# Query projection in two groups of row pairs a step, with two banks begun by their 128-row parts and the two sets of transposes in one pair of banks

## The chip, the cores and the metric

The kernel runs on one core of a Trainium2 chip. The metric is device time in microseconds (us) of one execution, as the median of several runs. The matrix engine is TensorE (PE in the profile, with PEld for its weight loads). VectorE (DVE) and ScalarE (ACT) do the elementwise work and empty the matrix engine's result banks (PSUM, eight banks). GpSimd (POOL) does a few small operations, and SyncE (SP) issues the DMAs. Each engine works through its own list of instructions in order, and semaphores tie the lists together.

## The reference

The input x has 2048 tokens of 448 numbers. A layer A (attention over segments, with a memory) and a layer B (a gated feed-forward) are applied twice in turn, each behind a layer norm and with a residual:

```python
for s in range(n_seg):                       # 64 segments of 32 tokens, one after the other
    h = concat([mem, xs])                    # 8 memory rows + 32 tokens = 40 rows
    q, k, v = h @ Wq, h @ Wk, h @ Wv         # 16 heads of 256
    p = softmax(where(mask, q @ k.T * scale, -1e9))
    o = (p @ v) @ Wo
    mem = o[:M]                              # the next segment's memory
    outs.append(o[M:])
...
x = x + A(layernorm(x)); x = x + B(layernorm(x))     # and both once more
B(x) = (max(x @ W_gate, 0) * (x @ W_up)) @ W_down
```

The memory makes each layer A a chain of 64 segments that can't run side by side. All four parts use the same weights A and B.

## The kernel before

At the start the kernel fuses Wq with Wk (tiles A_sb, A3, A3z) and Wv with Wo (B_sb) for every head. Attention then needs one "query" projection of a segment's rows, scores against the rows themselves, weighted sums of the rows (y, kept in tiles Y and Z), and one output projection (ox and o3).

**Steps.** The first A layer and the second one are two chains, the second four segments behind. `step(g, ff)` does segment g of chain 0 and segment g−4 of chain 1 together. There are 68 steps with work and a last short one. Steps 4 to 63 serve both chains (their rows stand side by side, 80 columns of a matmul); four steps at either end serve one chain (40 columns). Every second step also carries the feed-forward of a finished block (class `Feed`). In the middle of the run a step without the feed-forward takes 17.95 us and one with it 26.51 us.

**The query projection.** The 448 dims are cut into three chunks of 128 and a last one of 64. The result stands in PSUM banks named prj, class `Bank`: for each half hf of the heads (0 or 1) four banks i = 0 to 3 of six tiles each and a bank i = 4 of four tiles. I call half 0's banks b0 to b3 and z0, and half 1's c0 to c3 and z1, as the code does. Each tile takes three matmuls with all 128 rows (weights A_sb, "wide" from here on) and one with 64 rows for the last chunk (A3 or A3z). Two of the latter, on rows 0 to 63 and rows 64 to 127, run side by side on TensorE if they are issued one after the other: these are the row pairs. `open_banks` (L508) starts banks with their row pairs, and `close_bank` (L521) adds the wide matmuls and empties the bank: banks 0 to 3 go to the query tile TQ by one copy of VectorE or ScalarE, bank 4 goes to TZ in two, VectorE with partitions 0 to 63 first and ScalarE with 64 to 127.

**Other users of row pairs.** `flipped_dims` (L156) transposes with 64 rows each. It serves `hk_make` (L612), which turns the segment's rows hT into hk (eight transposes, banks kps, then copies by VectorE and ScalarE), and `Feed.residual` (L419), which turns the layer's outputs OT (eight transposes, banks otp). Of the two banks of a set, one comes from the pool tag "ox", which has one bank, and one from the pool tag "ps", which has seven and is used in turn. The output projection's bank ox has the tag "ox" as well, so a transposing set can begin only when ox has been emptied. The weighted sums y (`weigh_x`, the last thing that a step issues, 40 rows of each chain) are row pairs too.

**The end of a step.** `finish` (L736) empties ox: VectorE copies the memory columns to the next step's hT (L205), ScalarE copies the outputs of each chain to OT (L741, one copy for each chain, both on ScalarE). After it come the y matmuls of `weigh_x`, and their copies to Y or Z by both engines (L89 and L91, the lines of the helper `evac`).

**What sets the order.** On TensorE every matmul is chained to the one before (`in_order`), so that engine follows the program. On the other engines the tile framework's scheduler places the instructions, and the order in its list can differ from the program's.

The order of TensorE at the start of a step with both chains, with "|" where the form changes between row pairs and wide:

```
y, pairs of b0 b2 | wide b0, b2 | [transposes of OT, in a step with feed-forward] pairs of b1 b3 z0 z1
  | wide z0, b1, b3, z1 | transposes of hT (kps), pairs of c0 c2 c1 c3 | scores Sm of half 0, wide c0, c2, c1, c3
  transpose of the weights PM of half 0 (pps), scores Sx of half 0, weighted sum ya, ...
```

The scores Sm of half 0 need TQ and TZ of half 0. Behind them VectorE and ScalarE work out the softmax weights PM (maximum mx, difference and exponential se, sum, reciprocal, product), which TensorE transposes (pps), VectorE copies (PT), and ya reads.

Of the kernel before, what the change touches and what calls it, by code (L numbers as in the profile page):

```python
# [8 lines left out]
BF = mybir.dt.bfloat16  # L9
F32 = mybir.dt.float32  # L10
# [10 lines left out]
SEG = 32  # L21
L = MEM + SEG
# [9 lines left out]
HI = 128  # L32
HW = 5 * HI
W = 2 * L
XO = (0, 2 * L - SEG)
# [5 lines left out]
ROWS = (slice(0, 64), slice(64, 128))  # L41
# [7 lines left out]
def tidx(kd, eo, p4):  # L49

    return kd * 8 + eo * 4 + p4 if kd < 3 else 24 + p4


def build_kernel(ctx, tc, A_x, A_mem0, A_Wq, A_Wk, A_Wv, A_Wo, B_W_gate, B_W_up, B_W_down, out,
                 ntiles=16, nseg=64):
    nc = tc.nc
    P = nc.NUM_PARTITIONS
# [10 lines left out]
    psum = ctx.enter_context(tc.tile_pool(name="psum", bufs=7, space=bass.MemoryType.PSUM))  # L68
# [4 lines left out]
    def in_order(r):  # L73
        if last_pe[0] is not None:
            tc.add_manual_dep(r.ins, last_pe[0],
                              mybir.DependencyInfo(mybir.DependencyClass.NoSync,
                                                   mybir.DependencyReason.DATA),
                              reason="order of issue")
        last_pe[0] = r.ins.name

    def mm(*a, **k):
        in_order(nc.tensor.matmul(*a, **k))  # L82

    def tr(*a):
        in_order(nc.tensor.transpose(*a))  # L85

    def evac(eng, dst, src):
        if eng is nc.scalar:
            nc.scalar.copy(dst, src)  # L89
        else:  # L90
            eng.tensor_copy(dst, src)  # L91
# [8 lines left out]
    ident = glob.tile([P, P], BF, name="ident")  # L100
# [32 lines left out]
    A_sb = glob.tile([P, 3, 2, NT, 128], BF, name="A_sb")  # L133
# [5 lines left out]
    for i in range(2):  # L139
        t = glob.tile([P, BLK, HW], BF, name=f"hT{i}")  # L140
# [10 lines left out]
    for hf in range(2):  # L151
        t = glob.tile([P, 5, 6, 64], BF, name=f"TQ{hf}")
        tc.keep_in_program_order(nc.gpsimd.memset(t[:], 0.0))
        TQ.append(t)

    def flipped_dims(name, src):  # L156

        two = [psum.tile([P, 4, 64], BF, name=name, **where) for where in (dict(tag="ox", bufs=1), dict(tag="ps"))]
        for kd in range(4):
            for r in range(2):  # L160
                tr(two[r][:, kd, :], src(r, kd), ident[ROWS[r], ROWS[r]])
        return two

    def row_stats(t, pin=False):

# [220 lines left out]
    for hf in range(2):  # L386
        for name, shape, where in (("Y", [P, NT, W], YY[hf]), ("Z", [P, NT, W], YY[hf]), ("TZ", [P, 5, 128], TZ),
                                   ("PX", [P, 4, 64], PX), ("PM", [P, 2, 64], PM)):
            t = main.tile(shape, BF, name=f"{name}{hf}")
# [6 lines left out]
    OT = main.tile([P, 4, 128], BF, name="OT")  # L396
# [5 lines left out]
    for i in range(2):  # L402
        t = main.tile([P, 6, 128], BF, name=f"hk{i}")
# [4 lines left out]
    class Feed:  # L408


        def __init__(self, i):
            self.i = i
            self.first = i < nblk
            self.second = 0 <= i - LAG // BLK < nblk
            self.n = slice(0 if self.second else TB, P if self.first else TB)
            self.x = xa[i % 3]
            self.nx = xp[i % 2]

        def residual(self):  # L419
            tp = flipped_dims("otp", lambda r, kd: OT[ROWS[r], kd, :])  # L420
            xd = self.x[:].rearrange("p (c d) -> p c d", d=64)
            for r in range(2):
                nc.vector.tensor_tensor(xd[:, r::2, :], tp[r][:, 0:4 - r, :], xd[:, r::2, :], op=ALU.add)
            self.st = row_stats(self.x)
# [56 lines left out]
    def moving(hb, j, idx, chains, rows=slice(0, P)):  # L481

        if len(chains) == 2:
            return hb[rows, j, idx * HI:(idx + 1) * HI].rearrange("p (c k) -> p c k", k=64)[:, :, 0:L]
        c = chains[0]
        return hb[rows, j, idx * HI + 64 * c:idx * HI + 64 * c + L]

    class Bank:


        def __init__(self, hf, i):
            self.hf = hf
            self.i = i
            self.tiles = [tidx(kd, i // 2, 2 * (i % 2) + k) for kd in range(3) for k in range(2)] if i < 4 else                 list(range(24, NT))
            self.ps = psum.tile([P, 512], F32, tag="ps", name="prj")

        def out(self, t, n):
            k = self.tiles.index(t)
# [6 lines left out]
        kd, eo, p4 = t // 8, t // 4 % 2, t % 4  # L505
        return eo, A3[ROWS[eo], hf, 4 * kd + p4, :]

    def open_banks(chains, hb, j, *which):  # L508

        n = L * len(chains)  # L510
        banks = [Bank(hf, i) for hf, i in which]
        for a, b in zip(banks[::2], banks[1::2]):
            for k in range(len(a.tiles)):
                for bk in (a, b):
                    t = bk.tiles[k]
                    r, w = last_rows(bk.hf, t)
                    mm(bk.out(t, n), w, moving(hb, j, 3, chains, ROWS[r]), start=(k == 0), stop=False,
                       skip_group_check=True)
        return banks

    def close_bank(bk, chains, hb, j, eng):  # L521

        n = L * len(chains)
        hf, N = bk.hf, len(bk.tiles)
        for t in bk.tiles:
            for kd in range(3):
                mm(bk.out(t, n), A_sb[:, kd, hf, t, :], moving(hb, j, kd, chains), start=False, stop=(kd == 2),
                   skip_group_check=True)
        ps = bk.ps
        if bk.i < 4:  # L530
            at = 2 * (bk.i // 2) + bk.i % 2
            parts = [(eng, slice(0, P), TQ[hf][:].rearrange("p g (k b) w -> p g k (b w)", b=2)[:, :, :, 32 * at:32 * at + 32], 3)]
        else:
            parts = [(nc.vector, slice(0, 64), TZ[hf][0:64, :, 0:64].unsqueeze(2), 1),
                     (nc.scalar, slice(64, 128), TZ[hf][0:64, :, 64:128].unsqueeze(2), 1)]
        for eng, rows, T, K in parts:
            T = T.rearrange("p g k (t q) -> p k t g q", q=16)
            if len(chains) == 2:
                evac(eng, T, ps[rows, 0:N * n].rearrange("p (k t g q) -> p k t g q", k=K, t=N // K, q=16))
                continue  # L540
            c = chains[0]
            src = ps[rows, 0:N * n].rearrange("p (k t w) -> p k t w", k=K, t=N // K)
            x, m = (0, SEG) if c == 0 else (MEM, 0)
            evac(eng, T[:, :, :, 2, MEM * c:MEM * c + MEM], src[:, :, :, m:m + MEM])
            evac(eng, T[:, :, :, 3 * c:3 * c + 2, :],
                 src[:, :, :, x:x + SEG].rearrange("p k t (g q) -> p k t g q", q=16))

    def queries(hf, g, kd):
        return TQ[hf][:, g, 2 * kd:2 * kd + 2, :] if kd < 3 else TZ[hf][:, g, :]
# [47 lines left out]
    at = [0]  # L597

    def step(g, ff):
        chains = active(g)  # L600
        xs = active(g - 1)
        ms = [c for c in chains if g - c * LAG + 1 < nseg]
        gb, j = divmod(g, BLK)
        hb = hTb[gb % 2]
        cols = [(0, 32) if c == 0 else (48, 80) for c in xs] + [(32, 40) if c == 0 else (40, 48) for c in ms]
        lo, hi = min(a for a, _ in cols), max(b for _, b in cols)
        ox = None
# [1 line left out]
        def ys(hf, later=0):  # L609
            return YY[hf][(g + later) % 2]  # L610

        def hk_make():  # L612
            kps = flipped_dims("kps", lambda r, kd: hb[ROWS[r], j, kd * HI:kd * HI + HI])
            hk = HK[g % 2]
            for r, eng in enumerate((nc.vector, nc.scalar)):
                evac(eng, hk[:, 0:4, 64 * r:64 * r + 64], kps[r][:])
            nc.scalar.copy(hk[:].rearrange("p k n -> p (k n)")[:, 512:768].rearrange("p (a b) -> p a b", b=64)[:, 0::3, :],
                           kps[1][:, 3, :].unsqueeze(1).to_broadcast([P, 2, 64]))
            return hk
# [112 lines left out]
        def ot_cols(c):  # L732
            o = (g - 1) % BLK * SEG + (TB if c == 0 else 0)
            return OT[:, :, o:o + SEG]

        def finish():  # L736
            if ms:
                src = ox[:, :, M0:M0 + 16].rearrange("p k (c m) -> p k c m", m=MEM)
                set_mem(g + 1, src[:, :, ms[0]:ms[-1] + 1, :], ms, 3)
            for c in xs:  # L740
                nc.scalar.copy(ot_cols(c)[:, 0:3], ox[:, :, XO[c]:XO[c] + SEG])  # L741

        def feed(*us):
            if ff is not None:
# [3 lines left out]
        def load_some():  # L748
            if g < 3:
                for part in (2 * at[0], 2 * at[0] + 1):  # L750
                    if part < NPASS + FT // 2:
                        load_ff(part)
                at[0] += 1
# [7 lines left out]

        load_some()
        nc.gpsimd.tensor_copy(hb[ROWS[0], j, 4 * HI:4 * HI + 104], hb[ROWS[0], j, 3 * HI:3 * HI + 104])
        b0, b2 = open_banks(chains, hb, j, (0, 0), (0, 2))
        close_bank(b0, chains, hb, j, nc.vector)
        close_bank(b2, chains, hb, j, nc.scalar)
        if ff is not None:
            ff.residual()
            ff.norm(nc.gpsimd)
        b1, b3, z0, z1 = open_banks(chains, hb, j, (0, 1), (0, 3), (0, 4), (1, 4))  # L770
        close_bank(z0, chains, hb, j, None)
        load_some()
        close_bank(b1, chains, hb, j, nc.vector)
        close_bank(b3, chains, hb, j, nc.scalar)
        close_bank(z1, chains, hb, j, None)
        hk = hk_make()
        c0, c2, c1, c3 = open_banks(chains, hb, j, (1, 0), (1, 2), (1, 1), (1, 3))
        scores_m(0)
        close_bank(c0, chains, hb, j, nc.scalar)
        close_bank(c2, chains, hb, j, nc.scalar)  # L780
        close_bank(c1, chains, hb, j, nc.vector)
        close_bank(c3, chains, hb, j, nc.scalar)
# [63 lines left out]
    for g in range(nsteps + 1):  # L846
        if g == LAG - 1:
            set_mem(LAG, mem0T[:].unsqueeze(2), (1,))
        i = (g - 3) // 2
        step(g, Feed(i) if g % 2 and 0 <= i < nblk + LAG // BLK - 1 else None)  # L850

    ff = Feed(nblk + LAG // BLK - 1)
    ff.residual()
    ff.norm()
    ff.xposed()
# [62 lines left out]
```

## Time and profile before

| | us |
|---|---|
| runs shown: lowest, median, highest | 1580.89, 1584.73, 1585.72 |
| the profiled execution | 1579.01 |
| its span, from the first to the last instruction | 1576.9 |
| TensorE busy | 1547.3 |
| VectorE busy | 1112.7 |
| ScalarE busy | 783.3 |
| GpSimd busy | 174.9 |

The profiled execution took 2.1 us more than its span, and 5.7 us less than the median of the runs. The mean granted TensorE clock was 0.993 of full speed. In a list of instructions in order of time the columns are: start, time, engine, line, operation, tile written <- tiles read, shapes, and how many were merged into the row. Matmuls overlap, so the time of a group reads longer than the distance to the next group's start; the distances between starts are what counts. In the table of stages each engine has its busy time, then come the granted clock (PEclk), the DMA share and GB/s.

### The profile page before, as it was taken

Reading aid. Unit: us, or ns where it says so; the run is one execution under the profiler, and the core shown is the slowest. Engines: PE = TensorE matmul, PEld = TensorE weight load, DVE = VectorE, ACT = ScalarE, POOL = GpSimd, SP = SyncE. Lnnn points to the kernel's source line nnn. Section 1 sums busy time; section 2 is a strip of 40 time slices with the busy share of each in tenths; the row PEclk is TensorE's granted clock in tenths of the full one; section 3 lists DMA queues with packets and bytes.
Section 4 is the critical chain, followed back from the end, with each engine's and each line's share of the span. In section 5 each row is a group of like instructions: output and inputs, shape, how many; then the busy total and the mean of one; then the engine's idle time right before and its main releaser. Section 6 shows DMA issues by size and latency. Waiting matters only on the chain.

```text
span 1576.9 us, 98176 instructions
## 1 busy us (share of the span) xinstructions
PE 1547.3 (98%) x45116; PEld 1422.8 (90%) x45116; DVE 1112.7 (71%) x3825; ACT 783.3 (50%) x2307; POOL 174.9 (11%) x308
## 2 busy tenths in 40 slices
PE   8999999999999999999999999999999999999997
PEld 6588899999999999999999999999999999999886
DVE  6756777777777777777767677776777777776673
ACT  6634544554445544544445545554455545544442
POOL 3201111011001111011001111011011110111010
PEclk9989999999999999999999999999999999999999
DMA  9530000000000000000000000000000000000000
GB/s 285 149 80 9 9 10 8 6 10 10 10 10 10 10 10 8 6 9 10 10 10 10 10 10 5 8 10 10 10 10 10 10 10 5 9 8 7 7 7 6
DMA packets 29468, 33.12 MB, mean 21 GB/s; under 512 B 3320, under 2 KB 28160, under 8 KB 29056
## 3 DMA queue, kind: packets, MB, share of 16 engines
q1 hardware_dynamic: 28992, 26.85, 6.3%
q8 instruction: 352, 5.77, 1.5%
q14 instruction: 60, 0.49, 0.1%
q0 software_dynamic: 64, 0.01, 0.0%
HBM read 23.18 MB, written 1.84 MB: 16 GB/s over the span
## 4 chain that ended last, share of the span: by engine, by line
PE 94%; DVE 2%; ACT 1%; POOL 1%; issue 1%; DMA 0%; SPq 0%; POOLq 0%; ACTq 0%; DVEq 0%
PE prj L82 29%; PE ox L82 25%; PE ups L82 10%; PE dps L82 6%; PE o L82 5%; PE y L82 4%; PE Sx L82 3%; PE Sm L82 2%; PE bps L82 1%; PE pps L85 1%; PE gps L82 1%; PE aps L82 1%; PE tps L85 1%; PE kps L85 1%; PE ym L82 1%
## 5 line engine op out<-in xcount | busy, mean ns | idle before, releaser
L82 PEld LDWEIGHTS <-B_sb 128*128 128x128 bf16 (+1 forms) x15456 | 495.0, 103 | 29.2 <-issue 21.2
L82 PE MATMUL prj<-hT,A_sb 128*128 128x80 bf16 (+1 forms) x11424 | 430.6, 200 | 0.0
L82 PEld LDWEIGHTS <-A_sb 128*128 128x128 bf16 x11424 | 406.3, 100 | 8.3
L82 PE MATMUL ox<-Y,B_sb 128*128 128x80 bf16 (+4 forms) x5880 | 222.9, 199 | 1.9 <-DVE Y L650 1.9
L89 ACT CAST TQ<-prj 128x480 bf16<-128x480 f32 (+1 forms) x380 | 183.1, 494 | 82.8 <-PE prj L82 58.6
L82 PE MATMUL ox<-Z,B_sb 128*128 128x80 bf16 (+2 forms) x5712 | 217.7, 199 | 1.3 <-DVE Z L650 1.3
L82 PE MATMUL ups<-xT,Wgu_sb 64*128 64x128 bf16 (+1 forms) x3332 | 190.8, 214 | 1.3 <-DVE hh L447 0.8
L82 PE MATMUL gps<-xT,Wgu_sb 64*128 64x128 bf16 (+1 forms) x3332 | 190.9, 214 | 0.4 <-ACT xT L433 0.3
L82 PEld LDWEIGHTS <-Wgu_sb 64*128 64x128 bf16 x6664 | 179.1, 95 | 4.5 <-issue 2.5
L91 DVE CAST TQ<-prj 128x480 bf16<-128x480 f32 (+1 forms) x228 | 129.5, 574 | 17.3 <-PE prj L82 11.7
L447 DVE SCALAR_TENSOR_TENSOR hh<-gps,ut 128x256 bf16<-128x256 f32 (+1 forms) x238 | 94.7, 408 | 47.7 <-ACT ut L446 34.7
L446 ACT CAST ut<-ups 128x256 bf16<-128x256 f32 (+1 forms) x238 | 85.5, 359 | 82.1 <-PE gps L82 63.4
L89 ACT CAST Y<-y 64x128 bf16<-64x128 f32 (+2 forms) x256 | 89.4, 379 | 45.6 <-DVE Y L91 41.4
L91 DVE CAST Y<-y 64x128 bf16<-64x128 f32 (+2 forms) x256 | 102.1, 419 | 13.3 <-ACT Y L89 4.3
L89 ACT COPY hT<-tps 128x256 bf16<-128x256 bf16 x32 | 11.9, 372 | 197.8 <-DVE hT L91 197.8
L91 DVE CAST Z<-y 64x128 bf16<-64x128 f32 (+2 forms) x256 | 99.1, 418 | 12.4 <-ACT Z L89 5.5
L578 DVE COPY PT<-pps 128x128 bf16<-128x128 bf16 (+1 forms) x206 | 49.9, 256 | 80.3 <-PE pps L85 77.6
L89 ACT CAST Z<-y 64x128 bf16<-64x128 f32 (+2 forms) x256 | 89.2, 378 | 23.9 <-DVE Z L91 17.4
L89 ACT CAST TZ<-prj 64x320 bf16<-64x320 f32 (+2 forms) x152 | 56.1, 380 | 86.7 <-DVE TZ L91 78.7
L171 POOL TENSOR_SCALAR rstd<-mv 128x1 f32<-128x1 f32 x67 | 15.2, 227 | 729.2 <-DVE mv L169 729.2
L566 DVE TENSOR_REDUCE ssum<-se 128x2 f32<-128x80 f32 (+1 forms) x270 | 70.8, 274 | 35.7 <-ACT se L560 33.5
L82 PE MATMUL dps<-Wd_sb,hh 128*128 128x448 bf16 x476 | 96.0, 353 | 0.0
(130 smaller groups left out, 2342.1 us busy)
## 6 DMA issues: line engine op xcount, KB each, us to landing
wo<-in_A_Wo_dram SPq DMA_DIRECT2D x8, 448.0 KB, 7.7
nat<-in_A_Wq_dram SPq DMA_DIRECT2D x8, 384.0 KB, 6.2
nat<-in_A_Wk_dram SPq DMA_DIRECT2D x8, 384.0 KB, 6.4
nat<-in_A_Wv_dram SPq DMA_DIRECT2D x8, 384.0 KB, 7.2
xa<-in_A_x_dram SPq DMA_DIRECT2D x32, 56.0 KB, 2.8
xa<-xp SPq DMA_DIRECT2D x32, 56.0 KB, 1.9
out_dram<-xa SPq DMA_DIRECT2D x32, 56.0 KB, 2.0
xp<-in_A_x_dram SPq DMA_DIRECT2D x30, 56.0 KB, 2.1
```

Source lines behind the costliest of these rows:

```text
L82: in_order(nc.tensor.matmul(*a, **k))
L85: in_order(nc.tensor.transpose(*a))
L89: nc.scalar.copy(dst, src)
L91: eng.tensor_copy(dst, src)
L171: nc.gpsimd.tensor_scalar(out=rstd[:], in0=mv[:, 1:2], scalar1=EPS, scalar2=None, op0=ALU.add)
L446: nc.scalar.copy(ut[:, :, n], ups[:, :, n])
L447: nc.vector.scalar_tensor_tensor(out=hh[:, 2 * u:2 * u + 2, n], in0=gps[:, :, n], scalar=0.0, in1=ut[:, :, n], op0=ALU.max, op1=ALU.mult)
L566: nc.vector.tensor_reduce(ssum[:], se[:], axis=AX.X, op=ALU.add)
L578: nc.vector.tensor_copy(PT[:], pps[:].rearrange("p b q -> p (b q)"))
```

## The change

1. The transposes of hT and of OT move to the start of the step, behind the pairs of b0 and b2, and share one pair of banks (`flip_banks`: tiles of 8 slots, one bank of tag "ox" and one of "ps"). The copies to hk and the residual follow from there.
2. b1 and b3 are begun by their wide matmuls and finished by their row pairs. With that, all remaining row pairs (b1 b3, z0 z1, c0 c2, c1 c3) stand in one group. c0 takes the bank of tag "ox".
3. z0 and z1 are closed right behind that group. The scores Sm of half 0 stand in the middle of c0's wide matmuls (behind the first three of its six tiles).
4. In `finish`, the outputs of the second chain are copied to OT by VectorE and not by ScalarE.
5. The second call of `load_some` (feed-forward weights, only in the first three steps) comes behind `hk_make`.

The order of TensorE at the start of a step becomes:

```
y, pairs of b0 b2, transposes of hT, [transposes of OT] | wide b0, b2, b1, b3
  | pairs of b1 b3, z0 z1, c0 c2, c1 c3 | wide z0, z1, half of c0, scores Sm of half 0, other half of c0, c2, c1, c3
  transpose of PM (pps), Sx of half 0, ya, ...
```

```diff
-    def flipped_dims(name, src):
-        two = [psum.tile([P, 4, 64], BF, name=name, **where) for where in (dict(tag="ox", bufs=1), dict(tag="ps"))]
+    def flip_banks():
+        return [psum.tile([P, 8, 64], BF, name=f"flip{r}", **where)
+                for r, where in enumerate((dict(tag="ox", bufs=1), dict(tag="ps")))]
+
+    def flipped_dims(two, at, src):
         for kd in range(4):
             for r in range(2):
-                tr(two[r][:, kd, :], src(r, kd), ident[ROWS[r], ROWS[r]])
-        return two
+                tr(two[r][:, at + kd, :], src(r, kd), ident[ROWS[r], ROWS[r]])
+        return [t[:, at:at + 4, :] for t in two]
...
             for c in xs:
-                nc.scalar.copy(ot_cols(c)[:, 0:3], ox[:, :, XO[c]:XO[c] + SEG])
+                evac(nc.scalar if c == xs[0] else nc.vector, ot_cols(c)[:, 0:3], ox[:, :, XO[c]:XO[c] + SEG])
...
-        b0, b2 = open_banks(chains, hb, j, (0, 0), (0, 2))
+        b0, b2 = Bank(0, 0), Bank(0, 2)
+        pairs((b0, b2), chains, hb, j, True)
+        two = flip_banks()
+        kps = flipped_dims(two, 0, lambda r, kd: hb[ROWS[r], j, kd * HI:kd * HI + HI])
+        if ff is not None:
+            ff.flip_out(two)
         close_bank(b0, chains, hb, j, nc.vector)
         close_bank(b2, chains, hb, j, nc.scalar)
         if ff is not None:
             ff.residual()
             ff.norm(nc.gpsimd)
-        b1, b3, z0, z1 = open_banks(chains, hb, j, (0, 1), (0, 3), (0, 4), (1, 4))
+        hk = hk_make(kps)
+        load_some()
+        b1, b3 = Bank(0, 1), Bank(0, 3)
+        wide(b1, chains, hb, j, True)
+        wide(b3, chains, hb, j, True)
+        z0, z1 = Bank(0, 4), Bank(1, 4)
+        c0 = Bank(1, 0, tag="ox", bufs=1)
+        c2, c1, c3 = (Bank(1, i) for i in (2, 1, 3))
+        pairs((b1, b3), chains, hb, j, False)
+        leave_bank(b1, chains, nc.vector)
+        leave_bank(b3, chains, nc.scalar)
+        pairs((z0, z1, c0, c2, c1, c3), chains, hb, j, True)
         close_bank(z0, chains, hb, j, None)
-        load_some()
-        close_bank(b1, chains, hb, j, nc.vector)
-        close_bank(b3, chains, hb, j, nc.scalar)
         close_bank(z1, chains, hb, j, None)
-        hk = hk_make()
-        c0, c2, c1, c3 = open_banks(chains, hb, j, (1, 0), (1, 2), (1, 1), (1, 3))
+        wide(c0, chains, hb, j, False, slice(0, 3))
         scores_m(0)
-        close_bank(c0, chains, hb, j, nc.scalar)
+        wide(c0, chains, hb, j, False, slice(3, 6))
+        leave_bank(c0, chains, nc.scalar)
         close_bank(c2, chains, hb, j, nc.scalar)
```

`pairs` issues the row pairs of a list of banks, `wide` the 128-row matmuls of one bank, and `leave_bank` empties it; `close_bank` is `wide` and `leave_bank`.

More of the change, by code (lines that the diff above doesn't have):

```diff
@@ L417, in __init__, with flip_out @@
             self.nx = xp[i % 2]
+        def flip_out(self, two):
+            self.tp = flipped_dims(two, 4, lambda r, kd: OT[ROWS[r], kd, :])
         def residual(self):
-            tp = flipped_dims("otp", lambda r, kd: OT[ROWS[r], kd, :])
+            tp = self.tp
             xd = self.x[:].rearrange("p (c d) -> p c d", d=64)
@@ L488, in build_kernel, with __init__ @@
     class Bank:
-        def __init__(self, hf, i):
+        def __init__(self, hf, i, **where):
             self.hf = hf
@@ L494, in __init__ @@
             self.tiles = [tidx(kd, i // 2, 2 * (i % 2) + k) for kd in range(3) for k in range(2)] if i < 4 else                 list(range(24, NT))
-            self.ps = psum.tile([P, 512], F32, tag="ps", name="prj")
+            self.ps = psum.tile([P, 512], F32, name="prj", **(where or dict(tag="ps")))
         def out(self, t, n):
@@ L506, in last_rows, with pairs @@
         return eo, A3[ROWS[eo], hf, 4 * kd + p4, :]
-    def open_banks(chains, hb, j, *which):
+    def pairs(banks, chains, hb, j, opens):
         n = L * len(chains)
-        banks = [Bank(hf, i) for hf, i in which]
         for a, b in zip(banks[::2], banks[1::2]):
@@ L516, in open_banks, with wide, leave_bank @@
                     r, w = last_rows(bk.hf, t)
-                    mm(bk.out(t, n), w, moving(hb, j, 3, chains, ROWS[r]), start=(k == 0), stop=False,
+                    mm(bk.out(t, n), w, moving(hb, j, 3, chains, ROWS[r]), start=(opens and k == 0), stop=not opens,
                        skip_group_check=True)
-        return banks
-    def close_bank(bk, chains, hb, j, eng):
+    def wide(bk, chains, hb, j, opens, tiles=slice(0, 6)):
+        n = L * len(chains)
+        for t in bk.tiles[tiles]:
+            for kd in range(3):
+                mm(bk.out(t, n), A_sb[:, kd, bk.hf, t, :], moving(hb, j, kd, chains),
+                   start=(opens and kd == 0 and t == bk.tiles[0]), stop=(not opens and kd == 2),
+                   skip_group_check=True)
+    def leave_bank(bk, chains, eng):
         n = L * len(chains)
         hf, N = bk.hf, len(bk.tiles)
[L525 to L528, printed above, removed]
         ps = bk.ps
@@ L546, in close_bank @@
                  src[:, :, :, x:x + SEG].rearrange("p k t (g q) -> p k t g q", q=16))
+    def close_bank(bk, chains, hb, j, eng):
+        wide(bk, chains, hb, j, False)
+        leave_bank(bk, chains, eng)
     def queries(hf, g, kd):
@@ L610, in ys, with hk_make @@
             return YY[hf][(g + later) % 2]
-        def hk_make():
-            kps = flipped_dims("kps", lambda r, kd: hb[ROWS[r], j, kd * HI:kd * HI + HI])
+        def hk_make(kps):
             hk = HK[g % 2]
             for r, eng in enumerate((nc.vector, nc.scalar)):
-                evac(eng, hk[:, 0:4, 64 * r:64 * r + 64], kps[r][:])
+                evac(eng, hk[:, 0:4, 64 * r:64 * r + 64], kps[r])
             nc.scalar.copy(hk[:].rearrange("p k n -> p (k n)")[:, 512:768].rearrange("p (a b) -> p a b", b=64)[:, 0::3, :],
@@ L852, in build_kernel @@
     ff = Feed(nblk + LAG // BLK - 1)
+    ff.flip_out(flip_banks())
     ff.residual()
```

## The prediction

> **What bounds the kernel now.** I read the page first: busy times, then the chain that ended last.
>
> ```profile
> PE 1547.3 (98%) x45116; PEld 1422.8 (90%) x45116; DVE 1112.7 (71%) x3825; ACT 783.3 (50%) x2307; POOL 174.9 (11%) x308
> PE 94%; DVE 2%; ACT 1%; POOL 1%; issue 1%; DMA 0%; SPq 0%; POOLq 0%; ACTq 0%; DVEq 0%
> ```
>
> TensorE is the bound nearly everywhere. So an edit is worth what it does to the distances between TensorE's starts, and any wait that it gives TensorE counts in full. Next I read TensorE in order of time, from the border of two steps in the middle of the run:
>
> ```profile
> 809.55 0.61 PE L82 MATMUL y<-PT,hk 40*128 40x256 bf16 x8
> 810.03 0.39 PE L82 MATMUL prj<-hT,A 64*128 64x80 bf16 x12
> 810.36 1.46 PE L82 MATMUL prj<-hT,A_sb 128*128 128x80 bf16 x36
> 811.75 0.39 PE L82 MATMUL prj<-hT,A 64*128 64x80 bf16 x12
> 811.98 0.31 PE L82 MATMUL prj<-hT,A3z 64*128 64x80 bf16 x8
> 812.22 2.33 PE L82 MATMUL prj<-hT,A_sb 128*128 128x80 bf16 x60
> 814.47 0.29 PE L85 MATMUL kps<-ident,hT 64*128 64x64 bf16 x8
> 814.60 0.59 PE L82 MATMUL prj<-hT,A 64*128 64x80 bf16 x24
> 815.13 0.28 PE L82 MATMUL Sm<-hT,TQ 128*128 128x80 bf16 x3
> 815.24 0.20 PE L82 MATMUL Sm<-hT,TZ 128*128 128x80 bf16 x1
> 815.28 2.75 PE L82 MATMUL prj<-hT,A_sb 128*128 128x80 bf16 x72
> 817.86 0.22 PE L85 MATMUL pps<-ident,PM 128*128 128x128 bf16 x1
> ...
> 818.40 0.27 PE L82 MATMUL ya<-PT,hk 128*128 128x128 bf16 x2
> ```
>
> The 72 wide matmuls from 815.28 take 2.58 to the next start, 0.0358 each, with no row pairs at either end. The 36 from 810.36 take 1.39 where 36 × 0.0358 = 1.29: going over to row pairs costs 0.10. The 24 pair matmuls from 814.60 take 0.53, the 12 from 810.03 take 0.33: 0.0167 each, and 0.13 per group at its end, less the 0.0167 to 0.036 that a start takes anyhow. So one excursion into row pairs and back costs about 0.20.
>
> Then the two engines beside it, first at the border, then where z0 is emptied:
>
> ```profile
> 809.66 0.21 DVE L205 CAST hT<-ox 128x48 bf16<-128x48 f32 x1
> 810.01 0.69 DVE L91 CAST Y<-y 128x512 bf16<-128x512 f32 x1
> ```
>
> ```profile
> 809.90 0.24 ACT L741 CAST OT<-ox 128x96 bf16<-128x96 f32 x1
> ```
>
> ```profile
> 812.86 0.48 DVE L91 CAST TZ<-prj 64x320 bf16<-64x320 f32 x1 [0.50 <-PE prj L82]
> 813.38 0.42 ACT L89 CAST TZ<-prj 64x320 bf16<-64x320 f32 x1 [0.96 <-DVE TZ L91]
> ```
>
> The reader sees that OT is copied while y still runs and that VectorE starts y's copy 0.46 behind the first y. ScalarE's TZ copy waits for VectorE's: 0.64 + 0.52 + 0.42 = 1.58 from z0's first wide matmul (812.22) until TZ is whole. Now 2.9 us lie between that start and Sm.
>
> **The change part by part**, for the 60 steps with both chains (matmul counts stay the same):
>
> 1. *One excursion fewer.* Three groups of pairs become two: y, pairs of b0 b2 and the transposes; then everything else. OT's transposes already stood in a group, so steps with and without feed-forward save the same: −0.20.
>
> 2. *The transposes at the front wait for ox to be emptied.* Their first bank is ox's own, so they need both OT copies of the step before. In the changed program's order VectorE has: memory columns, y's first copy (128x512), and only then the second chain's OT copy; TensorE's first transpose waits for that one. VectorE can't start y's copy before 810.01. The next instruction starts 0.61 later (the first two y copies together take 1.02, the second alone 0.41), so the OT copy starts at 810.62. VectorE has no row for 128x96; its rows of 128x48 (0.21) and 128x256 (0.41, ya's copy) bound it, and I take 0.26, close to the smaller one, plus 0.05 until TensorE goes on (PT's copy ended at 818.34, ya started at 818.40). TensorE may start at 810.93. It gets there at 810.03 + 0.33 − 0.13 + 0.02 = 810.25. Stall 0.68; at the border of the other kind (y at 827.54, first pairs 827.98, y's copy 828.00) it is 0.72. I take +0.70. Queued behind the transposes is all of TensorE's step, nothing can fill it. The move of the copy to VectorE is what puts it behind y. Without the transposes at the front the OT copy would have until 811.75.
>
> 3. *TZ is late for Sm.* z0's closing now stands 33 wide matmuls ahead of Sm (z0 and z1 12 each, 9 of c0): 33 × 0.0358 = 1.18, and three Sm matmuls more, 1.30, to the matmul that reads TZ. TZ is whole at 1.58, read at 1.63. Stall +0.34. VectorE is free for it: b1's copy (0.66) ends 0.4 before.
>
> 4. *The softmax of half 0 loses its cover.* Times from z0's first wide matmul: Sm ends with a start at 1.63. Before, the exponential came 0.79 behind that (815.24 to 816.03): 2.42. In the changed order ScalarE has c0's copy in front of it. c0's second half runs 1.67 to 1.99, its copy starts at 2.20 and holds ScalarE 0.54 (816.21 to 816.77 for such a copy): exponential at 2.74. PM is finished 1.21 behind it (816.03 to 817.24), 3.95; TensorE has 63 wide matmuls from 1.67 and wants PM at 3.92, gets it at 4.00: +0.08. VectorE then copies c1 (0.66, from 3.90) in front of PT, which starts at 4.49, ends at 4.72; ya at 4.77. TensorE is there at 4.49: 0.28, of which 0.06 are paid now (Sx's last start 818.30, ya 818.40, some 0.03 would do). Net +0.22. Behind ya nothing gets later: c3's copy is done sooner, which gives back 0.05 in steps without feed-forward (Sm of half 1 starts 0.09 behind yb there, 0.03 in the other kind). Items 3 and 4: +0.62.
>
> 5. *At no cost.* b1 and b3 the other way round: same matmuls, same banks in turn. The hk copies and the residual (0.27 + 0.45 of VectorE) now fall beside 72 wide matmuls (2.58), the c0 pairs that need the bank come 3.2 us behind. GpSimd's norm follows VectorE's statistics, later by some 0.4, and has over 1 us before TensorE reads xn (POOL done 835.12, read at 836.67). load_some touches three steps; SP's queue has only these loads there, wanted steps later. Without this cover: the copies alone are 0.7 a step.
>
> Sum: 60 × (−0.20 + 0.70 + 0.62) = 60 × 1.12 = 67. In the eight one-chain steps both OT and TZ waits exist too (ScalarE's OT copy stands behind a y copy there now, 121.92 against pairs from 121.36), but a wait of 0.6 for a bank goes: between −2 and +10 together, I take +4. Against the profiled execution: 1579 + 71 = 1650. The median stood 5.7 above that execution, so the forecast for the median is **1655**.
>
> Bounds: OT copy 0.21 to 0.41 and hand-over, ±0.1; exponential ahead of c0's copy after all, −0.2; other waits of the same kind, +0.15. So 0.85 to 1.35 a step, 51 to 81, with the one-chain steps 1634 to 1676.
>
> A wait can do more than its length, as a table of stages shows:
>
> ```profile
> 69.00:88.00 19.00, 15.32 (x492) 13.89 (x491) 10.66 (x52) 6.21 (x27) 11.68 (x14) 0.81 0.59 147
> 105.00:121.00 16.00, 14.42 (x515) 13.30 (x511) 9.39 (x45) 7.12 (x29) 0.27 (x1) 1.00 0.12 33
> ```
>
> At 81% busy the granted clock fell (to half, from 80.9 to 94.6); at 90% with gaps of 0.4 to 0.6 it stayed full. The new gaps make some 93 to 95%. The Trainium skill, "TensorE: Matmul & The Clock Gate", section "A second HAM failure mode: psum-queue depth-cycling", says that short idle times between groups of matmuls can make the clock swing between half and full. By that rule the rival below would come true; the second row speaks against it here.
>
> **Rivals.**
> - *Only the front stalls.* TZ and the softmax stay covered, as they are today in every step (815.24 is no wait). Against it: 1.58 of measured copies in 1.30 of matmuls. 60 × 0.50 = 30: 1615. Chance 0.09.
> - *Faster.* The place is VectorE's OT copy. If it is done by 810.20, TensorE never waits at the front; it decides from there. That takes the copy ahead of y's (809.87 + 0.31 = 810.18). If TZ comes in time as well, the excursions remain: 68 × 0.20 = 14 less, 1571. Against it: the order in the program. Chance 0.04.
> - *The clock is gated in the steady steps.* A step with 5.6 us at half clock took 0.7 more (88.96 to 105.28 against 105.50 to 121.14), 0.12 per us; at most 0.5 per us where the columns bound it. A stretch as long as that (13.7) in every pair of steps: 30 × (1.7 to 6.8) on top, 1705 to 1860. Chance 0.03.
> - *More waits than I found*, 1676 to 1700: 0.04.
>
> The forecast's own case, 1634 to 1676, gets 0.80. "Front only" comes into the range: 1612 to 1680. About 0.3% is what a measurement can tell here: faster 0.04, same 0.01, slower 0.95.
>
> **What would show it.** After: waits of TensorE for VectorE's OT at each border, the first transpose some 1.38 behind the first y; a hole of 0.3 in front of Sm's TZ matmul, released by ScalarE; the exponential behind c0's copy, ya waiting for PT; two groups of pairs a step; steps of 19.0 and 27.6. Steps of 17.7 and 26.3 would prove me wrong.

## The result, and the profile after

The changed kernel takes 1642.49 us (median of 4 runs, 1641.46 to 1645.27) where the kernel before takes 1584.08 (four runs, one more than the three shown above; 1580.89 to 1585.72): a ratio of 1.0381, with a 95% interval of 1.0366 to 1.0395. It is slower. Forecast were 1655 and a range of 1612 to 1680. The profiled execution took 1641.81 with a span of 1640.0, so the span grew by 63.1. The granted clock was 0.993, as before.

First the page of the kernel after, the busy times and the chain that ended last.

```profile
PE 1561.9 (95%) x45116; PEld 1424.5 (87%) x45116; DVE 1117.8 (68%) x3885; ACT 763.7 (47%) x2247; POOL 174.9 (11%) x308
PE 79%; DVE 12%; ACT 4%; issue 2%; POOL 1%; DMA 0%; SPq 0%; ACTq 0%; POOLq 0%; DVEq 0%
```

TensorE has the same 45116 matmuls. Its share of the last chain fell from 94 to 79% and VectorE's rose from 2 to 12: 16% of that chain is now VectorE's and ScalarE's. The waits of TensorE name two places (total, times, longest).

```profile
PE flip L85 <- DVE OT L91: 31.4, 60, 0.6
PE Sm L82 <- ACT TZ L89: 11.9, 60, 0.2
```

Sixty times each, once for every step with both chains. These totals are too small for what they cost, since the ends of matmuls are modelled and a wait is counted from such an end. The distance from one start to the next tells the whole. In order of time, TensorE and then VectorE at the border of two steps (time, duration, engine, line, tile):

```profile
839.12 0.61 PE L82 MATMUL y<-PT,hk 40*128 40x256 bf16 x8
839.60 0.39 PE L82 MATMUL prj<-hT,A 64*128 64x80 bf16 x12
840.49 0.29 PE L85 MATMUL flip<-ident,hT 64*128 64x64 bf16 x8 [0.50 <-DVE OT L91]
```

```profile
839.23 0.21 DVE L209 CAST hT<-ox 128x48 bf16<-128x48 f32 x1
839.58 0.69 DVE L91 CAST Y<-y 128x512 bf16<-128x512 f32 x1
840.19 0.25 DVE L91 CAST OT<-ox 128x96 bf16<-128x96 f32 x1
```

The twelve pair matmuls of b0 and b2 take 0.19 from the first start to the last, yet the transposes start 0.89 after the first of them. VectorE copies OT between 840.19 and 840.44, behind y's copy, and TensorE goes on at 840.49. From the last pair matmul's start to the first transpose lie 0.70 in steps without feed-forward and 0.74 in steps with it. I set 0.026 against that, the distance from the last transpose to the first pair matmul in the kernel before, where nothing waits.

The second place, TensorE from z0's first wide matmul until ya, with ScalarE and VectorE beside it:

```profile
844.30 1.36 PE L82 MATMUL prj<-hT,A_sb 128*128 128x80 bf16 x33
845.49 0.27 PE L82 MATMUL Sm<-hT,TQ 128*128 128x80 bf16 x3
845.93 0.21 PE L82 MATMUL Sm<-hT,TZ 128*128 128x80 bf16 x1 [0.17 <-ACT TZ L89]
845.97 2.43 PE L82 MATMUL prj<-hT,A_sb 128*128 128x80 bf16 x63
848.24 0.22 PE L85 MATMUL pps<-ident,PM 128*128 128x128 bf16 x1
...
848.92 0.28 PE L82 MATMUL ya<-PT,hk 128*128 128x128 bf16 x2
```

```profile
845.46 0.85 ACT L89 CAST TZ<-prj 64x320 bf16<-64x320 f32 x2 [1.04 <-DVE TZ L91]
846.50 0.56 ACT L89 CAST TQ<-prj 128x480 bf16<-128x480 f32 x1 [0.20 <-PE prj L82]
846.96 0.27 ACT L575 ACTIVATE se<-se 128x80 f32<-128x80 f32 x1
```

```profile
847.93 0.24 DVE L586 TENSOR_TENSOR PM<-se,rs 128x80 bf16<-128x80 f32 x1
848.09 0.65 DVE L91 CAST TQ<-prj 128x480 bf16<-128x480 f32 x1
848.65 0.21 DVE L593 COPY PT<-pps 128x128 bf16<-128x128 bf16 x1
```

Three Sm matmuls take 0.11, the fourth starts 0.44 after the first: TZ is late. ScalarE's exponential stands behind c0's copy, and VectorE's PT behind c1's copy, so ya starts at 848.92 where the last Sx started at 848.67.

A step without feed-forward takes 18.88 (17.95 before), one with it 27.64 (26.51). These are medians over thirty steps of each kind, from a step's first row pair to the next step's: 30 × (0.93 + 1.13) = 62 of the 63 us that the span grew.

### The profile page after: what moved, and what is told of

The parts are those of the page before. It is cut to its first block, busy times and chain, and to the rows that moved or that the text cites. A ratio compares the mean times of both kernels' runs of the same rounds, so it can differ in the third digit from the quotient of the medians.

```text
span 1640.0 us, 98174 instructions
## 1 busy us (share of the span) xinstructions
PE 1561.9 (95%) x45116; PEld 1424.5 (87%) x45116; DVE 1117.8 (68%) x3885; ACT 763.7 (47%) x2247; POOL 174.9 (11%) x308
## 4 chain that ended last, share of the span: by engine, by line
PE 79%; DVE 12%; ACT 4%; issue 2%; POOL 1%; DMA 0%; SPq 0%; ACTq 0%; POOLq 0%; DVEq 0%
PE ox L82 24%; PE prj L82 18%; PE ups L82 10%; PE dps L82 6%; PE o L82 5%; PE y L82 3%; DVE TQ L91 2%; DVE TZ L91 2%; ACT TZ L89 2%; PE Sx L82 1%; PE flip L85 1%; ACT TQ L89 1%; PE Sm L82 1%; PE bps L82 1%; DVE Y L91 1%
## 5 line engine op out<-in xcount | busy, mean ns | idle before, releaser
L82 PEld LDWEIGHTS <-hk 40*128 40x128 bf16 (+1 forms) x1989 | 75.6, 95 | 24.9 <-DVE PT L593 10.6
```

## The experiments

The gaps below are distances between starts on TensorE: "front" from the last pair matmul of b0 b2 to the first transpose (0.026 without a wait), "TZ" from the third to the fourth Sm matmul of half 0 (0.036 without a wait), "pps" from the last wide matmul to PM's transpose (0.036), "ya" from the last Sx to ya (0.10 before). Two numbers are steps without and with feed-forward. Each ratio is to runs of the kernel before taken beside the run's own, whose medians lay between 1580.50 and 1584.08. e4, e7 and e8 change the kernel before and are told below.

| kernel | median us | ratio, interval | steps us | front | TZ | pps | ya |
|---|---|---|---|---|---|---|---|
| before | 1584.08 | | 17.95, 26.51 | none | 0.04 | 0.04 | 0.10 |
| after | 1642.49 | 1.038 [1.037, 1.040] | 18.88, 27.64 | 0.70, 0.74 | 0.37, 0.43 | 0.04, 0.08 | 0.25 |
| e1 | 1609.99 | 1.016 [1.013, 1.020] | 18.29, 27.05 | 0.11, 0.15 | as after | as after | as after |
| e2 | 1635.53 | 1.034 [1.031, 1.036] | 18.71, 27.42 | as after | 0.05, 0.11 | 0.18 | 0.26 |
| e3 | 1634.65 | 1.032 [1.030, 1.034] | 18.76, 27.44 | as after | 0.37, 0.43 | 0.04 | 0.11 |
| e5 | 1598.90 | 1.013 [1.011, 1.014] | 18.17, 26.84 | as e1 | as after | as e3 | as e3 |
| e6 | 1594.88 | 1.010 [1.008, 1.011] | 18.06, 26.83 | as e1 | 0.05, 0.11 | 0.12, 0.18 | 0.26 |
| e9 | 1575.62 | 0.995 [0.994, 0.997] | 17.82, 26.45 | 0.11, 0.15 | 0.04 | 0.04 | 0.10 |
| e10 | 1618.55 | 1.023 [1.022, 1.024] | 18.44, 27.20 | 0.26, 0.30 | as after | as after | as after |
| e11 | 1584.79 | 1.001 [1.000, 1.002] | 17.97, 26.59 | 0.26, 0.30 | 0.04 | 0.04 | 0.10 |

**e1, the OT copy back on ScalarE.** The changed kernel with both chains' outputs copied by ScalarE:

```diff
-                evac(nc.scalar if c == xs[0] else nc.vector, ot_cols(c)[:, 0:3], ox[:, :, XO[c]:XO[c] + SEG])
+                evac(nc.scalar, ot_cols(c)[:, 0:3], ox[:, :, XO[c]:XO[c] + SEG])
```

> The changed kernel with both OT copies on ScalarE again, ahead of its y copies. My theory (the front transposes wait for VectorE's OT copy behind y's copy): ScalarE's second OT copy starts 0.48 behind the first y and takes 0.25, TensorE can go on 0.78 behind it and arrives 0.66 to 0.70 behind it, so the hole of 0.71 in front of the transposes shrinks to about 0.1; steps of 18.27 and 27.03, time about 1606 us. Rival (the hole comes from the transposes' place behind the pairs and from ox's bank as such, whoever copies): the hole stays above 0.5, 1635 to 1645 us. The other holes (0.34 to 0.39 before the TZ matmul, 0.2 before ya) stay in both.

Measured: 1609.99, steps of 18.29 and 27.05, as the theory had it, and only the front gap changed. So 0.59 of the 0.93 and 1.13 a step belong to one line, the engine of a 0.25 us copy; putting the transposes in front costs 0.08 and 0.12 even so.

**e2, the scores behind the whole of c0.** TZ gets nine more wide matmuls of time.

```diff
-        wide(c0, chains, hb, j, False, slice(0, 3))
+        wide(c0, chains, hb, j, False)
         scores_m(0)
-        wide(c0, chains, hb, j, False, slice(3, 6))
         leave_bank(c0, chains, nc.scalar)
```

> The changed kernel with the scores Sm behind all six tiles of c0. Theory (one chain from z0's end through TZ, Sm, exponential, PM, c1's copy and PT to ya, which TensorE waits for wherever Sm stands): the hole before the TZ matmul falls from 0.34 to under 0.05, but a hole of about 0.1 comes in front of pps and ya still waits about 0.3; from z0's first wide matmul to ya 4.44 against 4.63, so 0.18 less a step, 1631 us. Rival (the waits are independent of each other, TZ's hole is given back in full): 0.36 less a step, 1621 us, ya's hole as it is.

Measured: 1635.53. The TZ gap fell by 0.32, and 0.10 to 0.14 of that came back in front of pps: TensorE gets there 0.32 sooner with nine matmuls less behind the scores, the exponential starts only 0.17 sooner (2.49 and not 2.66 behind z0's first wide matmul). The hole moves down its chain: z0, TZ, Sm, exponential, PM, pps. The steps fell by 0.17 and 0.22, near the theory's 0.18 and not the rival's 0.36.

**e3, the second half of c0 behind c2.** ScalarE then has the exponential ahead of c0's copy.

```diff
         scores_m(0)
+        close_bank(c2, chains, hb, j, nc.scalar)
         wide(c0, chains, hb, j, False, slice(3, 6))
         leave_bank(c0, chains, nc.scalar)
-        close_bank(c2, chains, hb, j, nc.scalar)
```

> The changed kernel with c0's second half behind c2, so that ScalarE has the exponential in front of c0's copy. Theory: TZ's hole stays at 0.34 to 0.39; the exponential comes about 0.23 earlier, PM no longer late, VectorE's copy of c1 is over when PT is due, and ya's hole of 0.22 shrinks to under 0.08: 0.15 to 0.18 less a step, 1632 us. Rival (ya's wait is due to VectorE's copy of c1 alone, whenever the exponential comes): ya's hole stays, 1642 us.

Measured: 1634.65; ya's gap went from 0.25 to 0.11 and pps' to its least, with TZ untouched. ScalarE in one of these steps, where TensorE read TZ at 843.33:

```profile
844.12 0.27 ACT L575 ACTIVATE se<-se 128x80 f32<-128x80 f32 x1 [0.42 <-DVE se L574]
844.42 1.02 ACT L89 CAST TQ<-prj 128x480 bf16<-128x480 f32 x2
```

The exponential starts 0.79 behind the TZ matmul (1.03 in the changed kernel, 0.79 in the kernel before), ahead of the copies. So it was c0's copy in front of the exponential that made PT late.

**e4, the OT copy alone.** The kernel before, with only the second chain's OT copy on VectorE:

```diff
-                nc.scalar.copy(ot_cols(c)[:, 0:3], ox[:, :, XO[c]:XO[c] + SEG])
+                evac(nc.scalar if c == xs[0] else nc.vector, ot_cols(c)[:, 0:3], ox[:, :, XO[c]:XO[c] + SEG])
```

> The kernel before, with the one edit that the second chain's OT copy is on VectorE (it stands behind y's first copy there too). Theory: nothing waits for it there, since OT's transposes come 2.16 behind the first y and the copy is done 1.33 behind it: within 0.3% of before, 1581 to 1588 us. Rival (the copy costs VectorE's chain its own 0.25 a step): 1600 us.

Measured: 1598.09, a ratio of 1.0094 [1.0071, 1.0117]. My theory, no difference, fell. Steps without feed-forward are unchanged (17.95), those with it take 27.05, 0.54 more, and the waits of TensorE have a new line:

```profile
PE prj L82 <- ACT Z L89: 10.2, 29, 0.4
```

It stands inside the row pairs of z0 and z1, whose eight starts take 0.66 instead of 0.11: z1's bank is one of y's. The rival's 1600 is near, but not its reason, 0.25 in every step. VectorE, ScalarE and TensorE there:

```profile
839.84 1.05 DVE L91 CAST Z<-y 64x128 bf16<-64x128 f32 x3
```

```profile
840.92 0.53 ACT L89 CAST Z<-y 64x128 bf16<-64x128 f32 x2 [1.12 <-DVE Z L91]
```

```profile
841.50 0.30 PE L82 MATMUL prj<-hT,A3z 64*128 64x80 bf16 x7 [0.35 <-ACT Z L89]
```

VectorE had copied memory columns, y, y, and then two small rests of y (64x128). With OT among them it takes the rests ahead of the second y. ScalarE's own rests wait for that second y, and TensorE for ScalarE. It is the new order of VectorE's list that costs here, more than the copy's 0.25.

**e5, both edits of e1 and e3.**

> The changed kernel with both edits of the first runs at once: both OT copies on ScalarE, and c0's second half behind c2. Theory (the front and the softmax chain are separate places, each with its own price): the two gains add, 0.59 at the front and 0.12 to 0.21 at ya; steps of 18.17 and 26.85, 1600 us. Rival (what is gained at the front is lost again further on): one gain alone, 1608 us or more.

Measured: 1598.90, steps of 18.17 and 26.84. The gains add, as the theory had it: 0.59 + 0.12 and 0.59 + 0.21.

**e6, the scores later still.** e5 with half of c3 in front of the scores too:

```diff
         wide(c0, chains, hb, j, False, slice(0, 3))
+        wide(c3, chains, hb, j, False, slice(0, 3))
         scores_m(0)
...
-        close_bank(c3, chains, hb, j, nc.scalar)
+        wide(c3, chains, hb, j, False, slice(3, 6))
+        leave_bank(c3, chains, nc.scalar)
```

> The changed kernel with both OT copies on ScalarE, and with the first halves of c0 and of c3 in front of the scores Sm, behind it c2, the rest of c0, c1, the rest of c3. So TZ has 42 wide matmuls of cover and the exponential still stands in front of c0's copy. Theory: TZ's hole closes (0.05 at most), PM is wanted 0.09 too early, PT waits for c1's copy: from z0's start to ya about 4.35, steps of 18.05 and 26.75, 1594 us, still not below before, since the chain from TZ to ya has no more work to cover it. Rival (with TZ covered nothing holds TensorE, and the saved excursion shows): steps of 17.8 and 26.4, 1575 us.

Measured: 1594.88, steps of 18.06 and 26.83. TZ is nearly in time, and pps and ya pay. With z0 begun only behind the big group of pairs, none of the three places of the scores that were tried serves both ends.

**e7, the price of an excursion.** The kernel before with OT's transposes taken out of their group and put among the wide matmuls, one more excursion in each of the 34 steps with feed-forward:

```diff
         close_bank(b0, chains, hb, j, nc.vector)
+        if ff is not None:
+            ff.tp = flipped_dims("otp", lambda r, kd: OT[ROWS[r], kd, :])
         close_bank(b2, chains, hb, j, nc.scalar)
```

> The kernel before, with OT's transposes moved between the wide matmuls of b0 and those of b2, so that they make an excursion of their own; nothing waits for them there (OT is finished 0.65 earlier). It measures the excursion alone. Theory: 0.20 more in each of the 34 steps with feed-forward and nothing in the others: 26.71 and 17.95, 7 us in all, 1589 us. Rival (the change of form costs nothing of its own; the distances around it are the eviction's): under 0.05 a step, 1583 us.

Measured: 26.72 against 26.51, so 0.21 an excursion, with no change in the other steps (17.95); the median is 1585.58, a ratio of 1.0042 [1.0028, 1.0057]. The Trainium skill, "TensorEngine Tiling (Array Packing)", section "Key Properties", says that a change of the tiling mode drains TensorE. A drain as such isn't seen in the trace, but 0.21 for a change and back agrees with one.

**e8, the OT copy on VectorE behind all of y's copies**, in the kernel before, to see whether that place is free:

```diff
-            for c in xs:
-                nc.scalar.copy(ot_cols(c)[:, 0:3], ox[:, :, XO[c]:XO[c] + SEG])
+            if xs:
+                nc.scalar.copy(ot_cols(xs[0])[:, 0:3], ox[:, :, XO[xs[0]]:XO[xs[0]] + SEG])
+
+        def finish_late():
+            for c in xs[1:]:
+                nc.vector.tensor_copy(ot_cols(c)[:, 0:3], ox[:, :, XO[c]:XO[c] + SEG])
...
             weigh_x(1, hk, px1)
+            finish_late()
```

> The kernel before, with the second chain's OT copy on VectorE, but behind all of y's copies and not behind the first. In the run with it behind the first, steps with feed-forward took 27.05 and not 26.51, with a wait of 0.55 for ScalarE's copies of y's last bank in front of the pairs of z1. Theory (VectorE's share of that bank is late there, and ScalarE's share waits for it; the copy itself costs nothing): the wait goes, 26.51 and 17.95, 1581 to 1585 us. Rival (any 0.25 more on VectorE at the border is paid): 1590 us or more.

Measured: 1590.22, a ratio of 1.0044 [1.0028, 1.0061]: the rival's number. The wait of e4 is gone, as the theory had it, and steps without feed-forward are unchanged, but those with it take 0.25 more. VectorE, then TensorE, in one of them:

```profile
878.29 1.52 DVE L91 CAST Z<-y 128x512 bf16<-128x512 f32 x4
879.82 0.26 DVE L745 CAST OT<-ox 128x96 bf16<-128x96 f32 x1
```

```profile
880.23 0.29 PE L85 MATMUL otp<-ident,OT 64*128 64x64 bf16 x8 [0.17 <-DVE OT L745]
```

Now OT itself is late for its transposes. So neither of the two places tried for this copy on VectorE is free. Beside the kernel before, e4 cost about 15 us and e8 about 7; in the changed kernel, where the transposes stand at the front of every step, the copy on VectorE costs 1642.49 − 1609.99 = 32.5.

**e9, z0 begun early.** All findings together: both OT copies on ScalarE as in e1; z0 begun by its wide matmuls with b1 and b3 and finished by the first pairs of the second group; half of c0 between z1 and the scores and its other half behind c2; ScalarE empties b3 ahead of its half of TZ. The lines of e1 and e3 and those that pin ScalarE's order are left out here.

```diff
+        wide(z0, chains, hb, j, True)
...
-        pairs((b1, b3), chains, hb, j, False)
-        leave_bank(b1, chains, nc.vector)
+        pairs((z0, z1, b1, b3, c0, c2, c1, c3), chains, hb, j, True, (z0, b1, b3))
         leave_bank(b3, chains, nc.scalar)
-        pairs((z0, z1, c0, c2, c1, c3), chains, hb, j, True)
-        close_bank(z0, chains, hb, j, None)
+        leave_bank(z0, chains, None)
+        leave_bank(b1, chains, nc.vector)
```

> Two groups of pairs, with the four findings built in: both OT copies on ScalarE; z0 begun by its wide matmuls with b1 and b3, so that it is complete at the first pairs of the second group and TZ is copied beside the rest of the group; behind the group z1 and half of c0, then Sm; c0's other half behind c2; and ScalarE empties b3 ahead of its half of TZ. Theory: from z0's completion TZ is whole 1.42 to 1.48 later, and TensorE reads it 1.61 later; no hole at TZ, pps or ya, only 0.08 to 0.12 at the front. So 0.20 saved less 0.10 lost, and the 0.05 of before at ya and at the second Sm gone: steps of 17.76 and 26.37, 1572 us, 0.6% below before. Rival (each cover that is taken opens another hole, as in the runs before): steps of 18.0 and 26.6 or more, 1585 us or more.

Measured: 1575.62 (5 runs, 1573.78 to 1577.26), a ratio of 0.9954 [0.9941, 0.9967]. That is 0.5% less than the kernel before, a small gain but clear of the noise. Steps take 17.82 and 26.45. ScalarE and TensorE in one without feed-forward:

```profile
811.97 0.42 ACT L89 CAST TZ<-prj 64x320 bf16<-64x320 f32 x1
```

```profile
812.44 0.27 PE L82 MATMUL Sm<-hT,TQ 128*128 128x80 bf16 x3
812.55 0.20 PE L82 MATMUL Sm<-hT,TZ 128*128 128x80 bf16 x1
```

TZ is whole at 812.39, and the fourth Sm matmul follows the third without a hole, 0.11 after the first. Beside e5, which has neither z0's early start nor ScalarE's new order, steps are 0.35 and 0.40 shorter, about the 0.34 and 0.39 by which TZ's gap was too long. What is left is the front gap, 0.11 and 0.15: one excursion saves 0.21, the gap gives back 0.08 and 0.12, which leaves 0.13 and 0.09; measured are 0.13 and 0.07. The theory had 0.19 and 0.14; the 0.05 that it hoped to win in front of ya did not come (0.10, as before).

**e10, the place and not the engine.** The changed kernel, with VectorE's OT copy held ahead of y's first copy (`r` is that copy of y):

```diff
+                if hf == 1 and c == 1 and t0 == 0:
+                    tc.keep_in_program_order(r)
...
-                evac(nc.scalar if c == xs[0] else nc.vector, ot_cols(c)[:, 0:3], ox[:, :, XO[c]:XO[c] + SEG])
+                if c == xs[0]:
+                    nc.scalar.copy(ot_cols(c)[:, 0:3], ox[:, :, XO[c]:XO[c] + SEG])
+                else:
+                    tc.keep_in_program_order(nc.vector.tensor_copy(ot_cols(c)[:, 0:3], ox[:, :, XO[c]:XO[c] + SEG]))
```

> The changed kernel with one difference: VectorE still copies the second chain's outputs to OT, but ahead of the first y copy and not behind it. My theory: the 0.71 in front of the transposes comes from the place of that copy in VectorE's order, not from its engine. VectorE is free at about 0.31 after the first y in the steps without feed-forward (839.43, the memory columns' copy done), the OT copy takes 0.25, so ox is empty 0.6 after the first y and TensorE, which arrives at 0.68, does not wait. The gap in front of the first transpose falls from 0.739 to between 0.03 and 0.06; the other gaps (0.34 to 0.39 in front of TZ, 0.15 in front of ya) stay. Steps 18.17 and 26.93, span about 1598, median about 1600. Rival: the place of the copy is not what counts, since y's copy now comes 0.1 late and VectorE hands over later in all that follows (banks of y for b1, b3, z0): then part of the 0.7 comes back as another wait and the steps stay above 18.4 and 27.2, span above 1612.

Measured: 1618.55, steps of 18.44 and 27.20, 0.44 less than after. The rival has the numbers, but not the reason: no other gap grew, and the front gap stopped at 0.26 and 0.30. Of the 0.59 that e1 gave back, the place makes 0.44 and the engine 0.15. VectorE, ScalarE and TensorE at one border:

```profile
846.00 0.21 DVE L209 CAST hT<-ox 128x48 bf16<-128x48 f32 x1 [1.00 <-PE ox L82]
846.51 0.26 DVE L760 CAST OT<-ox 128x96 bf16<-128x96 f32 x1 [0.31 <-ACT OT L758]
```

```profile
846.24 0.24 ACT L758 CAST OT<-ox 128x96 bf16<-128x96 f32 x1 [2.63 <-DVE hT L209]
```

```profile
846.82 0.29 PE L85 MATMUL flip<-ident,hT 64*128 64x64 bf16 x8
```

The two copies don't run side by side. ScalarE's waits for VectorE's memory columns, and VectorE's waits for ScalarE's: in this trace whoever reads the bank ox waits until the other engine has done with it. My theory fell at that step; it had the copies parallel. The Trainium skill, "PSUM — Partial Sum Buffer", section "PSUM bank collisions raise a hardware error", says that two engines must not touch one bank on the same partitions at once, reads included, and that the compiler's scheduler puts a dependency between them. This trace agrees, with 0.03 from the end of one copy to the start of the other.

**e11, e9 with the copy of e10.** VectorE's copy of b1 is held in program order as well.

> The kernel in which z0 is begun early (17.82 and 26.45 a step, 1571.5 of span, its only gap left 0.106 and 0.147 in front of the first transpose, where 0.026 is the least), with the second chain's OT copy given to VectorE ahead of y's first copy, so that the two OT copies run side by side. My theory: the gap falls to about 0.03 and 0.04, which gives 0.08 and 0.11 a step: steps 17.74 and 26.34, span 1566, median about 1570, 0.8 per cent below the kernel before. Rival: VectorE, later by 0.25 in all that follows, holds a bank of y or TZ: no step under 17.8 and 26.4, span 1571 or more.

Measured: 1584.79, a ratio of 1.0008 [0.9996, 1.0020]: all that e9 had won is lost. The steps are longer by 0.15 each, and so is the front gap (0.26 and 0.30 against 0.11 and 0.15). Two copies in turn on ScalarE take 0.38 together; one on each engine takes 0.24 + 0.03 + 0.26 = 0.53. The difference is the 0.15. The rival named another wait, which didn't come; the theory fell for the reason that e10 shows.

## Why the prediction was right

The sign, the places and the size came out; 1655 was 12.5 too much. By its steps, with a step's value without and with feed-forward:

1. *One excursion fewer*, forecast −0.20. e7 measured 0.21 for one, in steps with feed-forward; I take it for both kinds.
2. *The transposes at the front*, forecast +0.68 and +0.72. The gaps are 0.70 and 0.74 less 0.026: +0.67 and +0.71. The 128x96 copy, for which there was no row, took 0.25 (0.26 taken). e1 shows that 0.59 of it comes from the copy's move to VectorE, as the prediction argued, and e10 that 0.44 of this is its place behind y.
3. *TZ late*, forecast +0.34. Measured +0.34 and +0.39; the 0.05 in steps with feed-forward was not foreseen.
4. *The softmax's cover*, forecast +0.08 at pps, +0.22 at ya and −0.05 at the second scores in steps without feed-forward. Measured 0 and 0.05 at pps, 0.15 at ya, −0.06 and 0. This term was too large: c0's copy held ScalarE 0.46 before the exponential could start (846.50 to 846.96), not 0.54, so the exponential and PM came 0.08 earlier than forecast. c1's copy in front of PT started 0.11 earlier, and ya came 0.15 earlier. e3 shows that the mechanism was the one named.
5. *At no cost*: no run takes these edits apart from the rest, but they have little left to explain. −0.21 + 0.67 + 0.34 + 0.15 − 0.06 = 0.89 of 0.93, and −0.21 + 0.71 + 0.39 + 0.05 + 0.15 = 1.09 of 1.13; 0.04 a step stays open. In steps without feed-forward the two traces put it among the row pairs (0.02), between the last Sx and ox (0.02) and between ya's two matmuls (0.01).

That a step with feed-forward came out at 27.64 where 27.6 was forecast is partly luck: the unforeseen 0.05 at TZ and the open 0.04 made up for most of the softmax term that was 0.10 too large.

The 60 steps give 62 where 67 were forecast. The eight one-chain steps and the ends make about +1, forecast +4, inside the bounds of −2 to +10. The other 5 us of the miss are the 5.7 added to get from the profiled execution to the median: after's profiled execution lies 0.7 below its median, and that difference belonged to one run of the kernel before.

Two sentences of the prediction did not hold, without moving its number. "Without the transposes at the front the OT copy would have until 811.75" is true of OT, but e4 shows that the same copy then makes a bank of y late, at 0.54 in every second step. And the rival "faster" put its deciding point at a copy ahead of y, ready at 810.18; e10 shows that this copy waits for ScalarE's, and that TensorE still waits 0.23 and 0.27 then; with both copies on ScalarE (e1) 0.08 and 0.12 are left. The rival's price of 1571 was near what e9 took, 1575.62, where the front gap is small and TZ in time.

The rival of the gated clock did not come true. The row that it rests on, 81% busy at a clock of 0.81, mixes two stretches: 69 to 81 us, 69% busy at 1.00, and 81 to 95 us, busy throughout at 0.52. With the holes of 0.3 to 0.7 in every step, and TensorE 96% busy, the granted clock was 1.00 from 105 to 1400 us, as in the kernel before, so the swing between half and full that the Trainium skill, "TensorE: Matmul & The Clock Gate", section "A second HAM failure mode: psum-queue depth-cycling", tells of did not show here.

## What to carry to other kernels

A group of instructions that is moved forward takes its waits with it: look up which copies must empty the bank that it uses, on which engine, and behind what they stand there. Where one bank is emptied by several copies, count them one after the other, whichever engines they are on, unless the trace shows them side by side; here giving one to a second engine saved nothing and made two copies take 0.53 instead of 0.38. An accumulation in two parts, the slow-to-empty bank begun early and finished first, gives the time for emptying that a mere shift of its reader only moves further down the chain.

## What the runs showed of the hardware that was not expected

- In e10 three copies from one bank ran strictly in turn over two engines, with 0.03 between the end of one and the start of the next (846.21 to 846.24, 846.48 to 846.51). TZ's two halves do the same (VectorE ends, ScalarE starts 845.46), though they lie on different partitions; whether those two could run side by side wasn't tried.
- In steps with feed-forward ScalarE's TZ copy started 0.09 after VectorE's had ended, in the others 0.035. In the former its wait is for two semaphores and the trace has a separate wait instruction of 17 ns ahead of it, in all thirty. The difference is the 0.05 by which the TZ gap is larger there; that the second semaphore causes it was not tested.
